# An adaLN transformer block on one core: first norm in natural feature order, key and value weights reordered on PE, a new instruction order

## Chip, cores, metric

The kernel runs on 1 core of a Trainium2 chip. The metric is the device time of one execution in microseconds, the median of several runs. All times below come from those runs or from one profiled execution.

## What is computed

One transformer block on 2048 tokens of width 1024, in bf16, conditioned on a vector `c`:

```
mod = silu(c) @ w_mod                       # six vectors of 1024: sa, ca, ga, sb, cb, gb
h = layernorm(x) * (1 + ca) + sa
q = h @ wq   (32 heads of 32);  k = h @ wk;  v = h @ wv      # one key and value head for all
x = x + ga * (softmax(q k^T / sqrt(32)) v) @ wo
h = layernorm(x) * (1 + cb) + sb
out = x + gb * (silu(h @ w1) * (h @ w3)) @ w2                # inner width 3584
```

## The kernel before

**One static order.** The program describes the work as a graph of operations (`Graph.op`), each with its engine (or alternatives), a duration that the author wrote in, what it reads and writes, and a due value `vt`. `Placer` (lines 194 to 420) then plays the graph in planned time and takes, again and again, the operation that can start first; among those that can start about as early on an engine it takes the lowest due value. Out of this come five fixed instruction streams with semaphore waits. `PLAN` (line 115) is a table with one row for every 16 score steps. A row holds allowances for choosing an operation that starts a little later, a time within which PE shall not change between value runs and fill ("hold"), and additions to the due values by kind of work and engine ("q/pe", "ln/act" and so on). On the chip each engine keeps the order that the planner found, whatever the true durations are. If an operation has alternatives, the engine that can start it first in planned time gets it.

**Setup.** SP issues the loads in this order: token tiles 0 to 3, the first half of w_mod's scale columns (field 1), tiles 4 and 5, the second half, tiles 6 and 7, the first quarter of wq, tiles 8 to 11, the two halves of the shift columns (field 0), the rest of wq, tiles 12 to 15. ACT issues `c`, wk and wv. `WSPL = (0, 4, NC)` (line 589) sets where a field is cut: 8 chunks, 4 and 4.

The width of 1024 is spread over 128 partitions and 8 chunks. In the first norm, feature p*8 + c stands in partition p and chunk c (`pc`, line 573), so that wk and wv (64 bytes a row) can be loaded with 512 bytes a partition. w_mod is loaded in this way too, and so is wq.

- `lnt1` (line 640) handles one tile of 128 tokens: statistics on DVE, 1/sqrt on POOL, normalization on ACT (tiles 0 to 7) or DVE, 8 transposes on PE that take every eighth feature of `XN`, and a copy from PSUM to `HT` on ACT or DVE.
- `mod_cols` (line 673) makes a field's 1024 values as columns: 64 matmuls, for each of 8 chunks and 8 groups of outputs, whose weights are a strided slice of w_mod (every eighth column) and whose moving operand is silu(c), repeated 64 times. Field 1 becomes `MODC` (1 + ca), field 0 becomes `SAB` (sa).
- `scale0` (line 689) multiplies wk, wv (`WKS`) and the first part of wq (`WQ0S`) by 1 + ca. `k_bias` (line 703) makes the biases of K and of the first two groups of Q from `SAB`. `k_proj` (line 741) makes K for 256 tokens, four times over in the partitions, `q_proj` Q, `v_proj` V.
- Two groups of throw-away matmuls on `IDENT` (lines 1076 and 1092, 27 and 16 operations) stand at low priority in between.

**Main stage.** For each of 8 token blocks (256 tokens), 8 groups of 4 heads and 8 pairs of key tiles, `s_exp` (line 834) does a score step: 8 matmuls S (4 heads side by side on the array), then two exponentials on ACT from PSUM to a slot of `U`, a ring of 10 slots. For every 8 steps `av` (line 865) adds the slots up on DVE (pairs, then further levels in `PS`), runs 64 value matmuls over the 8 slots in one go (the value run, U and V), the sums through `ONES`, and normalizes on DVE into `QT`. Between S steps PE gets fill: Q projections, `mod_chunk`, wo (`wo`, line 928), and the feed-forward part (`slab`, `quarter`) of the block before. All fill goes through two PSUM banks, PB. A slot of U can be written again only when its value matmuls and its sums have read it.

**Second norm.** `wo` adds the attention output to x, norms it, and for blocks 1 to 6 transposes by DMA into `QT`; then 8 operations scale and shift the 8 chunks on DVE, planned at 0.17 us each. Blocks 0 and 7 transpose on PE instead.

**Tail.** After the last exponential: the last value run, wo, norm and feed-forward part of block 7.

In the profile nearly all instructions have line 22, a helper; so I name them by engine and tiles. `HT<-PB` on ACT is a tanh of the feed-forward part or, in setup, the copy of a norm.

Of the kernel before, what the change touches and what calls it, by code (L numbers as in the profile page):

```python
# [42 lines left out]
class Graph:  # L43
# [63 lines left out]
    def alias(self, new, old):  # L107
# [8 lines left out]
    (0.0, 0.12, 0.2, 1, 0.7,  # L116
     {"wo/pe": -19, "mc/pe": 25, "slab/dve": -28, "ln/dve": -40, "k/pe": 5, "mod/pe": 114, "mc/dve": 1}),
    (0.0, 0.12, 0.1, 1, 1.3, {"mc/pe": 27, "q/dve": -2, "ln/pe": 6, "ln/act": 32, "v/pe": 15, "mod/pe": 18}),
    (0.0, 0.12, 0.1, 1, 0.9,
     {"mc/pe": 27, "slab/act": -5, "q/dve": -2, "ln/pe": 6, "ln/act": 32, "v/pe": 15, "mod/pe": 18}),  # L120
    (0.0, 0.12, 0.1, 1, 0.9,
     {"q/pe": -119, "mc/pe": 27, "slab/act": -5, "q/dve": -2, "ln/pe": 6, "ln/act": 32, "v/pe": 15, "mod/pe": 18,
      "kb/pe": -44, "mc/dve": -51}),
    (0.0, 0.16, 0.2, 1, 2.6,
     {"slab/pe": -74, "q/pe": 2, "av/dve": 20, "slab/dve": 32, "slab/act": -7, "q/dve": -2, "mc/dve": 6}),
    (0.0, 0.16, 0.2, 1, 1.6,
     {"slab/pe": -74, "q/pe": 2, "av/dve": 20, "slab/dve": 32, "slab/act": -7, "q/dve": -2, "mc/dve": 6}),
    (0.0, 0.16, 0.2, 1, 1.3,
     {"slab/pe": -74, "q/pe": 2, "av/dve": 20, "slab/dve": 32, "slab/act": -7, "q/dve": -2, "mc/dve": 6}),
    (0.0, 0.13, 0.2, 1, 1.3,  # L130
     {"slab/pe": -74, "q/pe": 2, "av/dve": 20, "slab/dve": 32, "slab/act": -7, "wo/dve": 106, "q/dve": -2,
      "mc/dve": 6}),
    (0.0, 0.13, 0.2, 1, 1.3,
     {"slab/pe": -74, "q/pe": 2, "pair/dve": 22, "av/dve": 20, "slab/dve": 49, "slab/act": -7, "wo/dve": 106,
      "q/dve": -2, "mc/dve": 6}),
    (0.0, 0.11, 0.0, 1, 2.4, {"wo/pe": 4, "slab/pe": 107, "quarter/pe": -2, "q/pe": -26, "an/dve": 4, "q/dve": -119}),
    (0.0, 0.11, 0.02, 1, 2.6,
     {"wo/pe": 4, "slab/pe": 107, "quarter/pe": -2, "q/pe": -26, "an/dve": 4, "q/dve": -119}),
    (0.0, 0.11, 0.02, 1, 2.6,
     {"wo/pe": 4, "slab/pe": 107, "quarter/pe": -2, "q/pe": -26, "an/dve": 4, "q/dve": -119}),  # L140
    (0.0, 0.11, 0.2, 1, 2.6,
     {"wo/pe": 135, "quarter/pe": 20, "mc/pe": -8, "pair/dve": 119, "av/dve": -14, "an/dve": 72,
      "quarter/dve": -26, "wo/dve": 65, "q/dve": -66}),
    (0.0, 0.11, 0.2, 1, 1.4, {"wo/pe": -20, "slab/pe": 107, "q/pe": -26, "an/dve": 54, "q/dve": -119}),
    (0.0, 0.11, 0.02, 1, 3.1,
     {"wo/pe": -20, "q/pe": -26, "mc/pe": -3, "av/dve": 8, "an/dve": 54, "slab/dve": 29, "q/dve": -119}),
    (0.0, 0.11, 0.05, 0, 2.3,
     {"av/pe": -15, "q/pe": -9, "mc/pe": 109, "pair/dve": -1, "an/dve": 4, "slab/act": 15, "q/dve": 7,
      "mc/dve": 6}),
    (0.0, 0.11, 0.2, 1, 2.4,  # L150
     {"wo/pe": 17, "quarter/pe": -15, "mc/pe": -8, "pair/dve": -39, "av/dve": 1, "an/dve": 72,
      "quarter/dve": -26, "wo/dve": 65, "q/dve": -72}),
    (0.0, 0.12, 0.2, 1, 1.3, {"slab/pe": -12, "av/dve": 57}),
    (0.0, 0.11, 0.2, 1, 2.9,
     {"av/pe": -12, "wo/pe": -19, "slab/pe": -9, "quarter/pe": -39, "pair/dve": -2, "an/dve": -117,
      "quarter/dve": -16, "q/dve": -105}),
    (0.0, 0.11, 0.2, 1, 1.9,
     {"av/pe": -12, "wo/pe": -19, "slab/pe": -9, "quarter/pe": -39, "pair/dve": -2, "an/dve": -117,
      "quarter/dve": -16, "q/dve": -105}),
    (0.0, 0.11, 0.2, 1, 1.9,  # L160
     {"av/pe": -12, "wo/pe": -19, "slab/pe": -9, "quarter/pe": -39, "pair/dve": -2, "an/dve": -117,
      "quarter/dve": -16, "q/dve": -105}),
    (0.0, 0.11, 0.2, 0, 0.7,
     {"av/pe": -12, "wo/pe": -19, "slab/pe": -9, "quarter/pe": -39, "pair/dve": -2, "an/dve": -143,
      "quarter/dve": -16, "q/dve": -105}),
    (0.0, 0.11, 0.05, 1, 3.1,
     {"wo/pe": -17, "mc/pe": -8, "av/dve": 1, "an/dve": 47, "slab/act": 11, "quarter/dve": -26, "wo/dve": 86}),
    (0.0, 0.11, 0.05, 1, 3.1,
     {"wo/pe": -17, "mc/pe": -8, "av/dve": 1, "an/dve": 47, "slab/act": 11, "quarter/dve": -26, "wo/dve": 86}),
    (0.0, 0.11, 0.05, 1, 3.1,  # L170
     {"wo/pe": -17, "mc/pe": -8, "av/dve": 1, "an/dve": 47, "slab/act": 11, "quarter/dve": -26, "wo/dve": 86}),
    (0.0, 0.14, 0.2, 0, 0.1, {"slab/pe": -12, "pair/dve": -20, "av/dve": -18, "slab/dve": -24}),
    (0.0, 0.11, 0.05, 0, 3.3,
     {"wo/pe": -17, "mc/pe": -8, "pair/dve": 43, "av/dve": 14, "slab/act": 9, "quarter/dve": -26}),
    (0.0, 0.11, 0.05, 0, 3.3,
     {"wo/pe": -17, "mc/pe": -8, "pair/dve": 43, "av/dve": 14, "slab/act": 9, "quarter/dve": -26}),
    (0.0, 0.11, 0.2, 1, 1.4,
     {"av/pe": -15, "quarter/pe": -3, "q/pe": -9, "mc/pe": 33, "pair/dve": -16, "av/dve": -5, "an/dve": 18,
      "quarter/dve": -37, "q/dve": 7, "mc/dve": 6}),
    (0.0, 0.11, 0.2, 1, 1.4,  # L180
     {"quarter/pe": -3, "q/pe": -9, "mc/pe": 33, "av/dve": -5, "an/dve": 18, "quarter/dve": 74, "q/dve": 7,
      "mc/dve": 6}),
    (0.0, 0.11, 0.0, 1, 1.4,
     {"quarter/pe": -3, "q/pe": -9, "mc/pe": 33, "av/dve": -5, "an/dve": 18, "quarter/dve": 74, "q/dve": 7,
      "mc/dve": 6}),
    (0.0, 0.11, 0.05, 0, 4.1,
     {"wo/pe": -17, "slab/pe": -70, "mc/pe": -8, "pair/dve": 43, "av/dve": 14, "slab/dve": 97, "slab/act": 9,
      "quarter/dve": -26}),
    (0.0, 0.11, 0.2, 0, 3.3,
     {"slab/pe": -13, "quarter/pe": 27, "mc/pe": 61, "slab/dve": -16, "quarter/dve": 6, "wo/dve": 2}),  # L190
# [260 lines left out]
def build(nc, x_in, wq_in, wk_in, wv_in, wo_in, w1_in, w3_in, w2_in, c_in, wmod_in, out, S, D, F):  # L451
# [137 lines left out]
    WSPL = (0, 4, NC)  # L589
# [6 lines left out]
    def wq_dma(f0, f1, key, vt):  # L596
        dma("sp", WQ[:, :, f0 * P:f1 * P], pc(wq_in)[:, :, f0 * P:f1 * P], key, (f1 - f0) << 18, writes=[key], vt=vt,
            bw=FAST)
# [20 lines left out]
       reads=["C0", "C2"], writes=["C3"], vt=-1990)  # L619
    op("dve", lambda: [lambda e: e.tensor_copy(WKR[:, 0], WKV[:, 0].unsqueeze(2).broadcast_to([P, NC, 4, 32]))], 0.45,  # L620
# [19 lines left out]
    def lnt1(tt, vt):  # L640
# [286 lines left out]

    def wo(n, vt):
# [16 lines left out]
        if 0 < n < NB - 1:  # L945
# [169 lines left out]
    i = 0  # L1115
# [14 lines left out]
    for k, old in ((1, "WKR0"), (2, "WKR1"), (4, "SABR"), (6, "WQ0S"), (7, "WQ0S"), (5, ("XN", 2))):  # L1130
        G.alias([("PS", k)], [old])
# [73 lines left out]
```

## Time and profile before

| | us |
|---|---|
| median of 3 runs | 1142.18 (1142.15 to 1142.33) |
| profiled execution | 1142.53 |
| its span | 1140.70 |
| PE busy | 1115.7 (98%), 15538 matmuls |
| DVE busy | 953.9 (84%) |
| ACT busy | 1024.3 (90%) |
| POOL busy | 38.3 (3%) |
| exponentials (ACT, U<-S), 1024 | 962.8 busy |
| first exponential starts | 30.97 |
| last exponential ends | 1044.64 |
| granted PE clock | full in all slices |

Busy times of PE are no measure of its limit, since matmuls overlap and their ends are modelled; what counts is where it waits and who waits for it. The DMA share is the mean busy share of 16 DMA engines; it is near 1 in setup and 0.4 to 0.8 after it.

### The profile page before, as it was taken

What the parts mean: (1) busy time and instruction counts of PE and PEld (TensorE: products, weight loads), DVE (VectorE), ACT (ScalarE), POOL (GpSimd) and SP (SyncE); (2) the same over time, 40 slices, a digit from 0 to 9 for tenths busy, and PEclk for the clock granted to TensorE, in tenths of its full rate; (3) what the DMA queues carried; (4) which work ended last, traced back from release to release, by engine and by line L of the source; (5) the groups of instructions that cost most, each with busy time, mean ns of one, the idle gap of its engine ahead of it and who ended that gap; (6) DMA issues with size and microseconds to landing.
All of it is one profiled execution on the core that took longest, in us unless ns stands there. A gap on an engine that the chain in (4) does not pass through costs nothing.

```text
span 1140.7 us, 34695 instructions
## 1 busy us (share of the span) xinstructions
PE 1115.7 (98%) x15538; PEld 756.8 (66%) x15568; DVE 953.9 (84%) x1557; ACT 1024.3 (90%) x1161; POOL 38.3 (3%) x83
## 2 busy tenths in 40 slices
PE   8999999999999999999999999999999999999998
PEld 7644556666577756776567656776577656776887
DVE  7888899998888888888979799888978988888442
ACT  5999999999999999999999999999999999996110
POOL 4100000000000000000000010000100000000000
PEclk9999999999999999999999999999999999999999
DMA  9500379665596668665696659675686658667793
GB/s 345 179 2 1 113 222 245 181 187 155 132 264 194 172 163 221 191 196 154 145 253 196 173 143 236 192 204 131 156 249 192 174 140 231 194 188 202 222 291 118
DMA packets 374291, 209.45 MB, mean 184 GB/s; under 512 B 17536, under 2 KB 365952, under 8 KB 374144
## 3 DMA queue, kind: packets, MB, share of 16 engines
q1 hardware_dynamic: 373712, 207.11, 65.2%
q8 instruction: 122, 2.00, 0.8%
q14 instruction: 25, 0.20, 0.1%
q10 hardware_dynamic: 432, 0.13, 0.0%
HBM read 199.89 MB, written 4.19 MB: 179 GB/s over the span
## 4 chain that ended last, share of the span: by engine, by line
ACT 48%; PE 41%; DVE 8%; DMA 2%; issue 1%; SPq 0%; POOL 0%; DVEq 0%
ACT U L22 44%; PE PB L22 29%; PE S L22 12%; DVE PS L22 4%; ACT HT L22 4%; DVE QT L22 1%; DMA W<-in_A_wq_dram 1%; DVE HT L22 1%; DVE RB L22 1%; DVE X L22 0%; DMA QT<-XNB 0%; SPq L22 0%; DVE ST L22 0%; DVE XNB L22 0%; DVE RC L22 0%
## 5 line engine op out<-in xcount | busy, mean ns | idle before, releaser
L22 ACT ACTIVATE U<-S 128x1024 bf16<-128x1024 f32 x1024 | 962.8, 1105 | 15.7 <-PE S L22 7.7
L22 DVE TENSOR_TENSOR PS<-U 128x2048 bf16<-128x2048 bf16 x256 | 309.1, 1213 | 21.3 <-ACT U L22 19.2
L22 DVE TENSOR_TENSOR PS<-PS 128x1024 bf16<-128x1024 bf16 x368 | 248.9, 685 | 4.0
L22 PE MATMUL PB<-QT,W 128*128 128x256 bf16 x1856 | 230.6, 273 | 0.9 <-DVE RB L22 0.4
L22 PE MATMUL S<-QT,KT 32*128 32x256 bf16 x4096 | 203.4, 273 | 7.8 <-ACT U L22 5.5
L22 PEld LDWEIGHTS PB<-QT,W 128*128 128x128 bf16 x1856 | 169.9, 98 | 49.3 <-issue 26.8
L22 PE MATMUL PB<-W2S,HT 128*128 128x256 bf16 x1512 | 189.8, 273 | 0.0
L22 PEld LDWEIGHTS PB<-W2S,HT 128*128 128x128 bf16 x1512 | 136.9, 98 | 43.8 <-issue 27.2
L22 PEld LDWEIGHTS S<-QT,KT 32*128 32x128 bf16 x4096 | 60.7, 92 | 134.8 <-ACT U L22 122.4
L22 PE MATMUL PB<-U,V 128*32 128x256 bf16 x4032 | 125.6, 273 | 1.6 <-DVE HT L22 1.0
L22 PE MATMUL PB<-QT,HT 128*128 128x256 bf16 x960 | 120.6, 273 | 0.6 <-DVE HT L22 0.3
L22 PEld LDWEIGHTS PB<-U,V 128*32 128x32 bf16 x4032 | 99.7, 96 | 23.4 <-issue 10.8
L22 ACT ACTIVATE HT<-PB 128x512 bf16<-128x512 f32 (+1 forms) x110 | 76.4, 696 | 32.7 <-PE PB L22 32.6
L22 PEld LDWEIGHTS PB<-QT,HT 128*128 128x128 bf16 x960 | 87.7, 98 | 25.8 <-issue 14.0
L22 PE MATMUL PB<-HT,W 128*128 128x256 bf16 (+1 forms) x561 | 98.5, 316 | 2.4 <-issue 1.6
L22 DVE SCALAR_TENSOR_TENSOR HT<-HT,PB 128x512 bf16<-128x512 bf16 x102 | 69.4, 681 | 31.8 <-ACT HT L22 30.9
L22 DVE TENSOR_TENSOR HT<-HT,PB 128x512 bf16<-128x512 bf16 x102 | 69.5, 682 | 15.0 <-PE PB L22 13.2
L22 PEld LDWEIGHTS PB<-HT,W 128*128 128x128 bf16 x576 | 50.2, 97 | 37.0 <-issue 13.9
L22 PE MATMUL PB<-WO,QT 128*128 128x512 bf16 x217 | 54.0, 380 | 1.8 <-issue 1.3
L22 DVE STREAM_TRANSPOSE RB<-PB 128x256 f32<-128x256 f32 x63 | 28.2, 447 | 29.6 <-PE PB L22 29.4
L22 POOL TENSOR_SCALAR RS<-MV 128x1 f32<-128x1 f32 x32 | 11.3, 354 | 1015.4 <-DVE MV L22 1010.4
L22 DVE COPY RB<-PB 128x256 f32<-128x256 f32 x63 | 26.4, 419 | 18.5 <-PE PB L22 18.5
(112 smaller groups left out, 648.9 us busy)
## 6 DMA issues: line engine op xcount, KB each, us to landing
W<-in_B_w_dram SPq DMA_DIRECT2D x150, 512.0 KB, 4.9
W2S<-in_B_w_dram SPq DMA_DIRECT2D x28, 1792.0 KB, 8.3
HT<-in_B_w_dram SPq DMA_DIRECT2D x74, 512.0 KB, 4.9
W2S<-in_w_mod_dram SPq DMA_DIRECT2D x8, 1024.0 KB, 6.8
X<-in_A_x_dram SPq DMA_DIRECT2D x8, 512.0 KB, 6.3
U<-in_w_mod_dram SPq DMA_DIRECT2D x4, 1024.0 KB, 11.4
out_dram<-X SPq DMA_DIRECT2D x7, 512.0 KB, 7.9
U<-in_B_w_dram SPq DMA_DIRECT2D x1, 3584.0 KB, 14.0
```

What stands on the lines that cost most here:

```text
L22: return getattr(e, call[0])(*call[1], **call[2])
```

## The change

1. **Natural order in the first norm.** Feature c*128 + p now stands in partition p and chunk c. wq is loaded in that way (`cp`), the norm's transposes take 128 neighbouring columns, and `mod_cols` takes 128 neighbouring columns of w_mod as weights. Its planned duration goes from 0.482 to 0.23 a chunk. (w_mod's rows, the contraction over `c`, stay in the old order.)
2. **wk and wv** are still loaded in the old order. 8 + 8 transposes on PE put them into rows of 32 partitions, two copies on ACT or DVE with a strided read reorder them, 8 + 8 transposes bring them back, and one copy writes `WKV`. Banks 2, 3 and 4 and two tiles of `PS` serve as room for it.
3. **WSPL** is (0, 6, 8): the first load of a field has 6 chunks, the second 2.
4. **The second norm's 8 scalings** are planned at 0.258 us, and POOL is an alternative, planned at 0.8.
5. **PLAN** is another table, again with 33 rows; every row differs. The instruction order is thus made anew over the whole kernel.

```diff
-    dma("act", WKV[:, i], pc(w), ("WKV", i), 65536, writes=[("WKV", i)], vt=-1999)
+    dma("act", WKV[:, i], pc(w), ("WKV", i), 65536, writes=[("WKL", i)], vt=-1999)
...
-    WSPL = (0, 4, NC)
+    WSPL = (0, 6, NC)
...
-        dma("sp", WQ[:, :, f0 * P:f1 * P], pc(wq_in)[:, :, f0 * P:f1 * P], key, (f1 - f0) << 18, writes=[key], vt=vt,
+        dma("sp", WQ[:, :, f0 * P:f1 * P], cp(wq_in)[:, :, f0 * P:f1 * P], key, (f1 - f0) << 18, writes=[key], vt=vt,
...
+    WT = [PS[:, 3].rearrange("p h q -> p (h q)"), PS[:, 5].rearrange("p h q -> p (h q)")]
+    for i in range(2):
+        op("pe", lambda i=i: [lambda e, c=c: e.transpose(BANKH[2 + i][0:32, c * P:(c + 1) * P], WKV[:, i, c, :], IDENT[:])
+                              for c in range(NC)], 0.53, reads=[("WKL", i), "IDENT"], writes=[("S", 2 + i)], vt=-1990,
+           mode="F", post=0.145)
+        op("act", lambda i=i: [lambda e: e.activation(
+            WT[i][0:32, :].rearrange("p (q c) -> p q c", c=NC), BANKH[2 + i][0:32, :].rearrange("p (c q) -> p q c", q=P),
+            ACT.Copy)], 1.1, reads=[("S", 2 + i)], writes=["WT"] if i == 0 else ["WT1", ("XN", 2)], vt=-1990,
...
+    for i in range(2):
+        op("pe", lambda i=i: [lambda e, c=c: e.transpose(
+            BANKH[4][:, (8 * i + c) * 32:(8 * i + c + 1) * 32], WT[i][0:32, c * P:(c + 1) * P], IDENT[0:32, 0:32])
+            for c in range(NC)], 0.53, reads=["WT" if i == 0 else "WT1", "IDENT"] + ([] if i == 0 else [("XN", 2)]),
+           writes=[("S", 4)], vt=-1990, mode="F", post=0.145, waw=(i == 0))
+    op("act", lambda: [lambda e: e.activation(WKV[:], BANKH[4][:, 0:512].rearrange("p (s c f) -> p s c f", s=2, f=32),
+                                              ACT.Copy)], 0.6, reads=[("S", 4)], writes=[("WKV", 0), ("WKV", 1)], vt=-1990,
...
-                BANKH[b][:, cc * P:(cc + 1) * P], XN[slot].rearrange("p (q c) -> p c q", c=NC)[:, cc, :],
+                BANKH[b][:, cc * P:(cc + 1) * P], XN[slot][:, cc * P:(cc + 1) * P],
...
-                BANK[b][:, 64 * k:64 * k + 64], WM0[:, c, fld * D:(fld + 1) * D].rearrange("p (q k) -> p k q", k=NC)[:, k, :],
+                BANK[b][:, 64 * k:64 * k + 64], WM0[:, c, fld * D + k * P:fld * D + (k + 1) * P],
...
-                for c in range(WSPL[h], WSPL[h + 1]) for k in range(NC)], 0.482 * (WSPL[h + 1] - WSPL[h]), reads=["C3", ("WM0", fld, h)],
+                for c in range(WSPL[h], WSPL[h + 1]) for k in range(NC)], 0.23 * (WSPL[h + 1] - WSPL[h]), reads=["C3", ("WM0", fld, h)],
...
-                   0.17, reads=[("h2r", n, 0), ("h2r", n, 1), ("MODC", 3, cc // 4), ("MODC", 2, cc // 4)],
-                   writes=[h2k(n)[cc]], vt=vt)
+                   0.258, reads=[("h2r", n, 0), ("h2r", n, 1), ("MODC", 3, cc // 4), ("MODC", 2, cc // 4)],
+                   writes=[h2k(n)[cc]], vt=vt, alts=[("pool", lambda cc=cc: [lambda e: e.tensor_scalar(
+                       h2t(n)[:, cc, :], h2t(n)[:, cc, :], MODC[:, 3, cc:cc + 1], MODC[:, 2, cc:cc + 1], ALU.mult,
+                       ALU.add)], 0.8)] if POOLH else [])
```

One row of the table of before and one of after, the first of each:

```
    (0.0, 0.12, 0.2, 1, 0.7,
     {"wo/pe": -19, "mc/pe": 25, "slab/dve": -28, "ln/dve": -40, "k/pe": 5, "mod/pe": 114, "mc/dve": 1}),
...
    (0.2, 0.03, 0.0, 0, 1.4,
     {"q/pe": -9, "slab/act": -80, "wo/dve": -71, "ln/pe": -112, "ln/act": 31, "k/pe": 3, "k/dve": 33}),
```

More of the change, by code (lines that the diff above doesn't have):

```diff
@@ new lines @@
+    (0.0, 0.16, 0.02, 0, 0.7, {"wo/pe": 106, "q/pe": -45, "q/dve": -74, "ln/pe": -118, "ln/dve": 4, "mod/pe": -24}),
+    (0.0, 0.16, 0.02, 0, 0.7, {"wo/pe": 106, "q/pe": -45, "q/dve": -74, "ln/pe": -118, "ln/dve": 4, "mod/pe": -24}),
+    (0.2, 0.24, 0.2, 1, 0.6, {"q/pe": 47, "mc/pe": 46, "ln/act": -12, "k/pe": 22}),
+    (0.0, 0.12, 0.2, 0, 1.8,
+     {"wo/pe": -44, "quarter/pe": 47, "q/pe": 33, "mc/pe": 36, "pair/dve": -14, "wo/dve": -1, "ln/act": -12,
+      "k/pe": 22}),
+    (0.0, 0.11, 0.2, 1, 1.5, {"q/pe": 47, "mc/pe": 46, "av/dve": 6, "ln/act": -12, "k/pe": 22}),
@@ new lines @@
+    (0.0, 0.11, 0.2, 1, 1.9, {"q/pe": -13, "mc/pe": 46, "av/dve": 4, "ln/act": -12, "k/pe": 22}),
+    (0.0, 0.11, 0.2, 0, 3.4, {"wo/pe": 35, "an/dve": 55, "slab/dve": 1}),
+    (0.0, 0.11, 0.2, 1, 1.4, {"av/dve": -11, "an/dve": 55, "slab/dve": 1, "q/dve": 9}),
+    (0.0, 0.11, 0.1, 0, 2.4,
+     {"wo/pe": 14, "slab/pe": 12, "quarter/pe": 3, "q/pe": -6, "av/dve": 18, "an/dve": 69, "slab/act": -1,
+      "quarter/dve": -7}),
+    (0.0, 0.11, 0.05, 0, 2.4, {"slab/act": 6, "wo/dve": 53}),
+    (0.0, 0.11, 0.2, 0, 2.9, {"wo/pe": 46, "an/dve": 55, "slab/dve": -89, "q/dve": 67}),
@@ new lines @@
+    (0.0, 0.11, 0.2, 1, 1.3, {"wo/pe": -13, "pair/dve": 6, "an/dve": 55, "slab/dve": -89, "q/dve": 67}),
+    (0.0, 0.11, 0.1, 1, 2.7,
+     {"slab/pe": -132, "q/pe": 47, "mc/pe": 46, "pair/dve": -13, "av/dve": 23, "slab/dve": -39, "slab/act": -20,
+      "quarter/dve": -47, "ln/act": -12, "k/pe": 22}),
+    (0.0, 0.11, 0.1, 1, 2.3,
+     {"slab/pe": -132, "q/pe": 47, "mc/pe": 46, "pair/dve": -13, "av/dve": -84, "slab/act": -20,
+      "quarter/dve": -47, "ln/act": -12, "k/pe": 22}),
+    (0.0, 0.11, 0.2, 1, 4.1,
+     {"wo/pe": 138, "slab/pe": -132, "quarter/pe": 13, "q/pe": 47, "mc/pe": 46, "pair/dve": -13, "av/dve": -83,
+      "slab/dve": -39, "slab/act": -20, "quarter/dve": -47, "ln/act": -12, "k/pe": 22}),
@@ new lines @@
+    (0.0, 0.11, 0.2, 1, 1.3,
+     {"slab/pe": -124, "q/pe": 47, "mc/pe": 46, "pair/dve": -24, "av/dve": -89, "an/dve": -26, "slab/dve": -39,
+      "slab/act": -20, "ln/act": -12, "k/pe": 22}),
+    (0.0, 0.11, 0.05, 1, 3.7,
+     {"wo/pe": -5, "quarter/pe": 48, "pair/dve": -3, "av/dve": -2, "slab/act": -7, "wo/dve": 20}),
+    (0.0, 0.11, 0.05, 1, 3.7,
+     {"wo/pe": -5, "quarter/pe": 48, "pair/dve": -3, "av/dve": -2, "slab/act": -7, "wo/dve": 20}),
+    (0.0, 0.11, 0.2, 1, 2.6,
+     {"wo/pe": 112, "slab/pe": -124, "quarter/pe": 26, "q/pe": 20, "mc/pe": 46, "pair/dve": 13, "av/dve": -89,
+      "an/dve": -26, "slab/dve": -39, "slab/act": -20, "quarter/dve": 35, "wo/dve": -2, "ln/act": -12,
+      "k/pe": 22}),
@@ new lines @@
+    (0.0, 0.11, 0.2, 1, 1.3,
+     {"slab/pe": -124, "quarter/pe": 26, "q/pe": 52, "mc/pe": 46, "pair/dve": 13, "av/dve": -72, "an/dve": -26,
+      "slab/dve": -39, "slab/act": -20, "quarter/dve": 35, "wo/dve": -6, "ln/act": -12, "k/pe": 22}),
+    (0.0, 0.11, 0.05, 1, 2.6,
+     {"slab/pe": -124, "quarter/pe": 26, "q/pe": 20, "mc/pe": 46, "av/dve": -89, "slab/dve": -39,
+      "slab/act": -20, "quarter/dve": 35, "ln/act": -12, "k/pe": 22}),
+    (0.0, 0.11, 0.05, 1, 1.4,
+     {"slab/pe": -124, "quarter/pe": 26, "q/pe": 20, "mc/pe": 5, "av/dve": -89, "slab/act": -20,
+      "quarter/dve": 35, "ln/act": -12, "k/pe": 22}),
@@ L1129, in build @@
     G.alias([("PS", 0)], [("WKV", 0), ("WKV", 1), "WKS"])
-    for k, old in ((1, "WKR0"), (2, "WKR1"), (4, "SABR"), (6, "WQ0S"), (7, "WQ0S"), (5, ("XN", 2))):
+    for k, old in ((3, "WT"), (1, "WKR0"), (2, "WKR1"), (4, "SABR"), (6, "WQ0S"), (7, "WQ0S"), (5, ("XN", 2))):
         G.alias([("PS", k)], [old])
```

103 lines of the change are left out of this document (29 added, 74 removed).

## The prediction

> **What bounds the kernel now.** I read the windows view first, cutting the span where the exponentials begin and end (ACT, U<-S). Columns: stretch, its length, busy time of PE, PEld, DVE, ACT and POOL with instruction counts, PE clock, DMA share, GB/s.
>
> ```profile
> 0.00:31.00 31.00, 25.72 (x322) 22.61 (x323) 23.59 (x57) 18.70 (x20) 15.50 (x43) 1.00 0.97 342
> 31.00:200.00 169.00, 161.05 (x2463) 88.30 (x2478) 152.19 (x266) 168.13 (x187) 5.04 (x12) 1.00 0.42 125
> 200.00:400.00 200.00, 197.94 (x2848) 133.82 (x2847) 174.97 (x276) 196.52 (x226) 1.91 (x4) 1.00 0.67 184
> 400.00:600.00 200.00, 197.92 (x2763) 131.97 (x2766) 173.86 (x278) 195.33 (x223) 4.64 (x8) 1.00 0.70 189
> 600.00:800.00 200.00, 197.32 (x2837) 134.58 (x2839) 173.48 (x272) 195.00 (x221) 3.59 (x4) 1.00 0.66 180
> 800.00:1000.00 200.00, 198.02 (x2789) 133.74 (x2795) 175.46 (x282) 197.64 (x227) 6.06 (x8) 1.00 0.70 192
> 1000.00:1044.64 44.64, 44.59 (x656) 31.80 (x649) 40.64 (x61) 44.64 (x51) 0.00 (x0) 1.00 0.60 164
> 1044.64:1140.70 96.06, 93.12 (x881) 80.00 (x880) 39.66 (x70) 8.37 (x15) 1.58 (x4) 1.00 0.79 223
> ```
>
> The reader sees three stages. Setup (31.0 us) has its DMA share at 0.97. Main (1013.6 us) has ACT busy for 168.13 + 196.52 + 195.33 + 195.00 + 197.64 + 44.64 = 997.3 us, so it idles 16.4; PE is busy almost as long, and DVE is not the bound. In the tail (96.1 us) PE has all the work: its matmuls run end to end from 1061 on. So the end is the start of the exponentials + ACT's work + ACT's idle + the tail.
>
> Second, the timeline of setup: PE's rows, the cast that makes SAB, and the first exponential (start, length, engine, what, in brackets what it waited for). The DMA line is that of the two loads of shift weights; the later one was issued at 12.0 and has the largest of the three figures.
>
> ```profile
> 23.50 2.08 PE L22 MATMUL PB<-SCC,U 128*128 128x64 bf16 x32
> DMA to landing us min/median/max: 12.4/13.2/13.9
> 25.93 2.08 PE L22 MATMUL PB<-SCC,U 128*128 128x64 bf16 x32
> 28.14 0.11 DVE L22 CAST SAB<-PB 128x8 bf16<-128x8 f32 x1
> 28.60 0.66 PE L22 MATMUL PB<-SAB,W 128*128 128x64 bf16 x16
> 30.49 0.40 PE L22 MATMUL S<-QT,KT 32*128 32x256 bf16 x8
> 30.97 1.93 ACT L22 ACTIVATE U<-S 128x1024 bf16<-128x1024 f32 x2
> ```
>
> The second half of the shift weights lands at 12.0 + 13.9 = 25.9, and PE starts on it at 25.93. From there to the first exponential there is a single chain: 32 matmuls, the cast, the bias matmuls, the bias, K and Q, the scores. That chain, and not the norm, starts the main stage.
>
> Third, where ACT idles in the main stage. Its gaps listed one by one come to 14.8 us in 18 places; three of them, 2.69 us before 301.00, 2.38 before 587.14 and 1.65 before 622.33, wait for PE's PB matmuls. PE and ACT around the first:
>
> ```profile
> 298.92 1.70 PE L22 MATMUL PB<-W2S,HT 128*128 128x256 bf16 x14
> 300.55 1.93 PE L22 MATMUL PB<-U,V 128*32 128x256 bf16 x64
> 301.00 1.94 ACT L22 ACTIVATE U<-S 128x1024 bf16<-128x1024 f32 x2 [2.69 <-PE PB L22]
> ```
>
> The exponential at 301.00 had its scores (S ran at 297.65). It waited for a free slot of U, and the 64 value matmuls that read the oldest slots were put behind 14 feed-forward matmuls. The other two gaps have the same shape (26 and 22 fill matmuls, then the 64). So the main stage loses time where the order on PE puts a value run late.
>
> **The change, part by part.** The profiled execution took 1142.53 us (span 1140.70, 1.83 around it); the median of the runs is 1142.18, so I add up against 1142.53 and take 0.35 off.
>
> (a) Modulation columns, packed weights and a 6:2 split. Packed and strided loads stand beside each other in the groups:
>
> ```profile
> L22 PEld LDWEIGHTS PB<-SCC,U 128*128 128x128 bf16 x128 | 8.1, 165 | 0.9 <-DMA U<-in_w_mod_dram 0.9
> L22 PEld LDWEIGHTS PB<-SCC,W2S 128*128 128x128 bf16 x256 | 8.6, 98 | 1.7 <-issue 1.3
> ```
>
> The U form is strided by 8 elements, the W2S form packed, with the same 128 x 64 matmul behind both. In busy time a strided one costs 8.1/128 = 63 ns, a packed one 8.6/256 = 34. After the change the last piece holds 2 of 8 chunks, so 2 x 8 = 16 matmuls come after the landing. The first piece, 6 chunks, lands when 0.52 MB are still to come, at the 374 to 379 GB/s of that time 1.4 us earlier, at 24.5; its 48 packed matmuls take 48 x 34 ns = 1.6 and end at 26.1, a little past the landing. Sixteen packed matmuls of this shape took 0.66 (at 28.60): 26.8, and the cast 0.13 behind as now, at 26.9 instead of 28.14: -1.2 us. The bytes ahead of the landing are the same, in descriptors of the same length, so I leave 25.9 as it is. Bounds: -1.4 (PE done with the 48 at the landing) and 0.
>
> [...]
>
> (b) First S. K and Q are ready at 29.97, but PE does another K projection from 29.51 until S at 30.49, so a new order can gain up to 0.5 here; I take -0.2. Against (a) and (b) stands what comes next: the last two K blocks need token tiles 12 to 15, whose load was issued at 16.8 and lands 15.8 later, at 32.6, and their S steps run at 43.10 and 44.94. An earlier ACT could run dry there. From tile 12's landing to its K block I count 0.1 + 1.3 (statistics, two tiles: +1.5) + 0.2 + 1.0 (POOL) + 0.5 + 0.5 + 1.0 + 1.05 + 0.5, about 40.3, and the S that needs it ran at 43.1. So 2.8 us of room. Setup in sum: -1.4, from 0 (room not used) to -1.9.
>
> (c) Key and value weights: 32 transposes, three copies. Eight norm transposes take 0.5 us on PE, so 2.0 us; PE fills that time with 48 throw-away matmuls until 8.4, which hide them. The copies cost by the nearest rows 1.02 + 1.02 + 0.6 = 2.6 us on ACT (0.67, 0.67, 0.67 on DVE). The loads land at 4.9 and 6.8, the chain of the second ends near 10, and its first reader runs at 14.20: 4 us of cover. ACT idled 3.98 us before its first norm at 7.63. Value 0, bounds 0 and +2.6 (if the copies push the norms back one for one and these become last).
>
> (d) Norm transposes, packed: in busy time 72 ns a load against the 34 above, but the matmul behind takes 56 to 62. 128 of them gain at most 128 x 6 ns = 0.8 us on a PE that waits for loads: 0.
>
> (e) Second norm's scaling: 48 operations, on DVE or POOL, planned at 0.258 (0.17 before).
>
> ```profile
> 308.11 2.13 DVE L22 TENSOR_SCALAR QT<-QT,MODC 128x256 bf16<-128x256 bf16 x8
> 17.87 1.95 POOL L22 TENSOR_SCALAR PS<-W,MODC 128x256 bf16<-128x256 bf16 x2 [2.20 <-DMA W<-in_A_wq_dram]
> ```
>
> On DVE 2.13/8 = 0.266 each, on POOL 1.95/2 = 0.98 for the same shape. The planner gives an operation to whoever starts first, so POOL takes about 2 of 8 (1.95 us) while DVE does 6 (1.6): the block is ready in 2 us as now. DVE loses 12 x 0.266 = 3 us of work that bounds nothing. Value 0. Bounds: -1 (the order fits the true 0.266), +11 if POOL took 4 of 8: 4 x 0.98 - 2.13 = 1.8 us late, six blocks.
>
> (f) The new order. The table again has 33 rows; what it does in the main stage cannot be read off. The nearest rows are the kernel's own five stretches from 31 to 1000: idle 0.9, 3.5, 4.7, 5.0, 2.4 (standard deviation 1.7, so sqrt(5) x 1.7 = 3.8 on their sum). An order of the same quality would give 16.4 +/- 3.8; the ends are 0 idle (-16.4) and every stretch like the worst (5 x 5.0 = 25, +8.6). I take -2.4, one late value run fewer, because two durations that the planner had wrong (0.17 for 0.266; 1.93 for 2.08) are now near the rows, and such an order slips less on the chip.
>
> (g) Tail. The 448 + 224 feed-forward matmuls of the last block (0.109 each, 73.2 us) and what must come before them do not change. What could go is 1.0 us (the last value run starts at 1045.66, behind fill, where its exponentials end at 1044.64) and 0.7 (six left-over matmuls at 1102); what could come is more left-over fill, 18 matmuls for 2 us. Value 0, bounds -1.7 and +2.
>
> Sum: -1.4 - 2.4 = -3.8, so 1138.7 for a profiled execution and 1138.4 for the median.
>
> **Rivals.** 0.2% is 2.3 us, about what a measurement of this kernel can tell from no change: faster is below 1139.9, slower above 1144.5.
>
> Rival 1. Order much better: main idle halves, -8.2 - 1.4, so 1132.6. For it: the gaps are few and large. Against: PE is busy 198 of 200 us, with little room to move fill.
>
> Rival 2. Nothing arrives: the setup gain is given back at the later K blocks, or the new order costs what setup gains: 1140.8 to 1142.2. For it: a spread of 3.8 in (f) is larger than the gain.
>
> Rival 3. Slower by late value runs: each costs (2.69 + 2.38 + 1.65)/3 = 2.2 us, where 14 or more fill matmuls stand between an S and a value run while U is full. The new order is made anew everywhere, so it can have more than three. It decides from two more: 1142.2 - 1.4 + 4.4 = 1145.2; three more, 1147.4.
>
> Rival 4. Slower by POOL blocking DVE. If a POOL scaling shuts DVE out, 12 x 0.98 = 11.8 us are lost and 3.2 saved, at six places where PE waits for this very block: 1142.2 - 1.4 + 8.6 = 1149.4. Against: beside the two POOL operations at 17.87 six DVE scalings took 1.71 us, where eight alone take 2.13 (six, 1.6): 0.1 lost, not 1.95. [...]
>
> **Chances.** Forecast 0.50 (1136 to 1139.9), rival 1 0.16, rival 2 0.20, rival 3 0.09, rival 4 0.05. Faster: 0.50 + 0.16 + 0.01 of rival 2 = 0.67; the same 0.19; slower 0.14. The range takes in rivals 1 and 2 and the worse half of (f): 1132.6 to 1144.5; it leaves out the slower cases and a little beyond rival 1.
>
> **What to look for.** Right if the SAB cast falls near 26.9, the first exponential near 29.6, the strided loads' mean of 165 ns is gone, ACT's idle between first and last exponential is near 14, and the tail stays at 96. Wrong if the cast is late (landing moved, or PE behind the new transposes), if an exponential waits between 36 and 45 us, if more than three gaps wait for a value run, or if the DVE operations beside POOL's scalings stretch.

## The result, and the profile after

The changed kernel took 1134.4 us (median of 4 runs, 1133.84 to 1134.48), the kernel before 1142.16 beside it: a ratio of 0.9931, 95% interval 0.9916 to 0.9947, so 7.8 us less. The forecast was 1138.4. In what follows PE is the matrix engine, ACT ScalarE, DVE VectorE and POOL GpSimd; a score step, or S, is the group of matmuls that feeds two exponentials, and a value run the 64 matmuls that read eight slots of `U`. The profiled execution has a span of 1132.6 us against 1140.70.

The windows view of the changed kernel, cut again where its exponentials begin and end (same columns as in the prediction):

```profile
0.00:30.61 30.61, 23.94 (x354) 19.18 (x355) 22.94 (x57) 20.85 (x23) 15.83 (x43) 1.00 0.98 345
30.61:200.00 169.39, 163.05 (x2484) 87.51 (x2486) 151.42 (x265) 168.66 (x188) 6.23 (x12) 1.00 0.43 125
200.00:400.00 200.00, 198.53 (x2867) 135.79 (x2868) 177.18 (x276) 198.42 (x227) 4.95 (x6) 1.00 0.68 185
400.00:600.00 200.00, 199.21 (x2838) 134.59 (x2837) 176.01 (x279) 197.27 (x225) 10.10 (x12) 1.00 0.71 192
600.00:800.00 200.00, 199.51 (x2807) 134.49 (x2804) 176.20 (x274) 197.27 (x225) 5.77 (x8) 1.00 0.68 185
800.00:1000.00 200.00, 199.28 (x2869) 137.18 (x2866) 176.13 (x278) 198.63 (x229) 9.37 (x11) 1.00 0.70 190
1000.00:1036.50 36.50, 36.45 (x518) 25.86 (x516) 32.42 (x51) 36.50 (x42) 0.00 (x0) 1.00 0.60 164
1036.50:1132.60 96.10, 93.16 (x882) 80.04 (x880) 39.61 (x70) 8.36 (x14) 1.59 (x4) 1.00 0.81 223
```

Setup is 0.4 us shorter (30.97 to 30.61) and the tail is what it was (96.06, now 96.10). The main stage fell from 1013.67 to 1005.89. ACT's busy time in it is 168.66 + 198.42 + 197.27 + 197.27 + 198.63 + 36.50 = 996.75, as before (997.3); its idle time fell from 16.4 to 9.1. The gain is idle time of ACT in the main stage: -7.3, with -0.4 at the start and -0.5 of ACT work. The -0.4 is no more than the scatter of single profiles, as b_pool below shows.

What ACT's exponentials waited for in the main stage (us in total, times, longest), first in the kernel before, then in the changed one:

```profile
ACT U L22 <- PE S L22: 7.7, 14, 1.4
ACT U L22 <- PE PB L22: 6.7, 3, 2.7
```

```profile
ACT U L22 <- PE S L22: 8.8, 8, 1.4
```

The three waits for late value runs (PB) are gone. What is left are six gaps of 1.36 us, one in each of blocks 2 to 7. The first of them, in the timeline of the changed kernel:

```profile
278.73 0.40 PE L22 MATMUL S<-QT,KT 32*128 32x256 bf16 x8
279.06 1.48 PE L22 MATMUL PB<-W2S,HT 128*128 128x256 bf16 x12
280.47 1.93 PE L22 MATMUL PB<-U,V 128*32 128x256 bf16 x64
282.33 0.40 PE L22 MATMUL S<-QT,KT 32*128 32x256 bf16 x8
282.78 1.02 ACT L22 ACTIVATE U<-S 128x1024 bf16<-128x1024 f32 x1 [1.36 <-PE S L22]
```

Between two S steps stand 12 fill matmuls and a value run, 3.4 us, in which ACT uses up its scores. The value run is on time here; it is the next S that comes late.

From the first exponential of a token block to that of the next, in us (blocks 0 to 6), worked out from counts of the exponentials:

```
before   123.15 124.95 128.37 127.00 130.29 127.81 125.39
after    123.09 125.70 126.13 126.13 126.19 126.13 126.13
```

The new order does the same thing in every block from the third on, to within 0.1 us; the old one varied by 5 us.

The setup rows that answer to those in the prediction:

```profile
23.50 0.62 PE L22 MATMUL PB<-IDENT,XNB 128*128 128x128 bf16 x8 [0.60 <-ACT XNB L22]
25.54 2.16 PE L22 MATMUL PB<-SCC,U 128*128 128x64 bf16 x64 [0.29 <-ACT HT L22]
27.50 0.19 DVE L22 BATCH_NORM_AGGREGATE MV<-ST 128x2 f32<-128x12 f32 x1
27.74 0.17 DVE L22 CAST SAB<-PB 128x8 bf16<-128x8 f32 x1
30.61 1.93 ACT L22 ACTIVATE U<-S 128x1024 bf16<-128x1024 f32 x2
```

A packed shift matmul takes 2.16/64 = 34 ns, as forecast from the packed rows. But all 64 ran in one go from 25.54, and the cast came at 27.74, not at 26.9.

### The profile page after: what moved, and what is told of

It is laid out like the page before. It is cut to its first block, busy times and chain, and to the rows that moved or that the text cites. A ratio compares the mean times of both kernels' runs of the same rounds, so it can differ in the third digit from the quotient of the medians.

```text
span 1132.6 us, 34805 instructions
## 1 busy us (share of the span) xinstructions
PE 1113.1 (98%) x15600; PEld 754.6 (67%) x15600; DVE 951.9 (84%) x1544; ACT 1026.0 (91%) x1165; POOL 53.8 (5%) x95
## 4 chain that ended last, share of the span: by engine, by line
PE 63%; ACT 31%; DVE 4%; DMA 1%; issue 0%; POOL 0%; SPq 0%; DVEq 0%
PE PB L22 47%; ACT U L22 30%; PE S L22 16%; DVE PS L22 2%; DMA W<-in_A_wq_dram 1%; ACT HT L22 1%; DVE HT L22 1%; DVE RB L22 0%; SPq L22 0%; DVE ST L22 0%; DVE W L22 0%; ACT XNB L22 0%; POOL PS L22 0%; DVE XNB L22 0%; POOL RS L22 0%
## 5 line engine op out<-in xcount | busy, mean ns | idle before, releaser
L22 PE MATMUL PB<-HT,W 128*128 128x256 bf16 (+1 forms) x576 | 101.8, 318 | 1.0 <-DVE HT L22 0.6
L22 PE MATMUL PB<-WO,QT 128*128 128x512 bf16 x232 | 57.3, 381 | 0.0
L22 ACT ACTIVATE HT<-S 128x512 bf16<-128x512 f32 (+1 forms) x15 | 10.9, 736 | 30.5 <-PE S L22 30.5
```

The lines of the kernel that those rows point to most:

```text
L22: return getattr(e, call[0])(*call[1], **call[2])
```

## The experiments

The theory to be tested (theory 1 in the expectations): the gain is the order of PE's instructions in the main stage, and it holds only for the graph it was planned for. Its main rival there (theory 3): the edited operations (packed loads, scalings on POOL) bring the gain in any order. Besides, each term of the sum was tried alone. Where it says "order fixed", the planner's order was recorded and the program written out in that order with one edit; the figures in brackets behind a time are its ratio to the kernel before, measured beside it, and the 95% interval of that ratio. The kernel after has 1134.4 and a ratio of 0.9931. It ran only beside the first measurement of before, 1142.16; beside the experiments before took 1142.21 (the two tables, a_respaced, a_late_runs), 1142.62 (a_scal_dve, a_strided, a_split44, a_no_reorder) and 1142.61 (the other four). So a difference from 1134.4 below about 0.5 us says nothing, and the ratios are the safer guide.

**Table and graph exchanged.** The kernel before with the new table, and the changed kernel with the old one.

```diff
 # b_new_table, in the kernel before
-PLAN = [ 33 rows of before ]
+PLAN = [ 33 rows of after ]
```

> The kernel before with the new table alone, all else as before; the planner makes a new order from it. Theory 1 (the gain is this one order in the main stage, and a table is worth something only with the graph and durations it was found for): the order it gives leaves 102.3 us of planned PE work after the last score step where before has 96.1, and has 17 stretches with a value run that are over 2.3 us long, where before has five over 3; at 1 to 2 us each and 6 us of tail this is 1155 to 1170. Theory 2 (the new table is the better one by itself): about 1135. Theory 3 (the gain is the new setup and the true durations, whatever the table): about 1142.

Measured: 1172.51 (ratio 1.0265, 1.025 to 1.028), 2.5 above the range that theory 1 gave. ACT idles 36.3 us in its main stage, where before has 16.4, and the tail takes 103.1 us.

```diff
 # a_old_table, in the kernel after
-PLAN = [ 33 rows of after ]
+PLAN = [ 33 rows of before ]
```

> The changed kernel with the old table: natural order, packed weights, 6:2 split, transposes of the key and value weights, scalings at 0.258 and on POOL all stay. Theory 1 (the gain is this one order): the order it gives leaves 115.5 us of planned PE work after the last score step (96.1 in both kernels), so the tail is about 19 us longer while the main stage has 19 us less fill and can end earlier only as far as ACT allows (about 8 us at most): 1143 to 1155. Theory 3 (the gain is the new setup and the true durations, whatever the table): about 1134 to 1137.

Measured: 1161.18 (1.0164, 1.0149 to 1.0179), also beyond the range that theory 1 gave. Here ACT idles 16.3 us, as in before, and the tail takes 116.2 us, 20 more than in either kernel. Either mixture is 19 to 38 us slower than either kernel. So the edited operations do not bring the gain whatever the order (theory 3 falls as the whole cause), and neither of these two tables is worth anything away from its graph.

**The twelve scalings back on DVE** (a_scal_dve, order fixed).

```diff
 # the 12 operations that the planner gave to POOL (chunks 1 and 5 of six blocks)
-n.alt = 1   # pool
+n.alt = 0   # dve, in the planned sequence
```

> The changed kernel's order, held fixed, with the 12 second-norm scalings that run on POOL put back on DVE at the same place. My reading of the change (POOL's share bounds nothing): 1134.4 within 0.5. Rival (taking 3 us off DVE, or getting the block's first chunks earlier, is part of the gain): +2 to +4 us. Rival (POOL shuts DVE out while it runs): the kernel gets faster without it, by up to 8 us.

Measured: 1136.76 (0.995, 0.9935 to 0.9965), 2.4 us slower than after, or 2.2 by the ratios. That alone is little more than the two intervals allow, but the trace bears it out: blocks of 126.5 instead of 126.13, and 11.3 us of idle time on ACT in the main stage instead of 9.1. The waits of ACT, the place in the timeline where the wait arises, and the same place in after:

```profile
ACT U L22 <- PE S L22: 11.0, 14, 1.4
```

```profile
438.20 0.68 DVE L22 SCALAR_TENSOR_TENSOR HT<-HT,PB 128x512 bf16<-128x512 bf16 x1
438.94 1.93 PE L22 MATMUL PB<-U,V 128*32 128x256 bf16 x64 [0.34 <-DVE HT L22]
440.80 0.40 PE L22 MATMUL S<-QT,KT 32*128 32x256 bf16 x8
441.25 1.02 ACT L22 ACTIVATE U<-S 128x1024 bf16<-128x1024 f32 x1 [0.36 <-PE S L22]
```

```profile
437.75 0.68 DVE L22 SCALAR_TENSOR_TENSOR HT<-HT,PB 128x512 bf16<-128x512 bf16 x1
438.48 1.93 PE L22 MATMUL PB<-U,V 128*32 128x256 bf16 x64
```

The two extra scalings (0.53 us) hold up DVE's SCALAR_TENSOR_TENSOR from 437.75 (in after) to 438.20. That operation empties a PB bank, the value run waits for the bank, S stands behind the value run, and ACT runs dry for 0.36 us: six times 0.36 is the 2.2 that its waits grew by. DVE is idle for 12% of the block and still sets the end here.

**The same edit the other way round** (b_pool, the kernel before, order fixed).

```diff
 # chunks 1 and 5 of the eight scalings, six blocks
-q["dve"]
+q["pool"]
```

> The kernel before in its own order, with chunks 1 and 5 of the eight scalings in each of six blocks moved from VectorE to GpSimd, as after has them. If moving them is worth the 2.2 us that the reverse edit cost in after wherever it is done: 1140.0. If the worth came only from after's order, which was planned around the shorter VectorE work: within 0.6 of before, 1141.6 to 1142.8. If GpSimd's slower scalings (about 1.1 us each) come late for the fill that reads them: 1143 to 1146.

Measured: 1140.97 against 1142.61 (0.9985, 0.9976 to 0.9995), so -1.6, with an interval from -0.6 to -2.7: in the old order, too, the scalings on POOL are worth something, with no table made for them. ACT's waits in it:

```profile
ACT U L22 <- PE PB L22: 6.7, 3, 2.7
ACT U L22 <- PE S L22: 6.1, 9, 1.4
```

S waits fell by 1.6 and the three late value runs stayed. With this, -1.6 to -2.4 of the 7.8 belong to the scalings. What the order is worth without POOL stands in a_scal_dve, which has the new order and all scalings on DVE: against before it is 5.7 us faster (0.995), and ACT's idle time is 11.3 instead of 16.4. So about -5 of the main stage's gain is the order's.

This run also shows how far single profiles of one setup differ, for its setup is that of before, unchanged:

```profile
27.85 0.11 DVE L22 CAST SAB<-PB 128x8 bf16<-128x8 f32 x1
30.69 1.93 ACT L22 ACTIVATE U<-S 128x1024 bf16<-128x1024 f32 x2
```

In before's own profile these stood at 28.14 and 30.97. With after's setup, the first exponential starts at 30.61 in after, 30.33 in a_scal_dve and 30.86 in a_respaced_less. So the 0.4 us between before and after at the start of the exponentials cannot be told from nothing.

**Late value runs** (a_late_runs, order fixed, one in each of six blocks; the score steps after each are spaced anew).

```diff
 # PE, at six value runs
-S, 64 value matmuls, S, fill and S ...
+S, 12 fill matmuls, 64 value matmuls, S, fill and S ...
```

> The changed kernel's order, held fixed, with one edit on PE: six value runs in mid-block (heads' groups 20, 28, 36, 44, 52, 60) are put behind 12 fill matmuls that stood after them, and the score steps after them are spaced so that nothing else moves. This puts back, six times, the shape of the three long gaps of the kernel before (2.69, 2.38, 1.65 us of ACT idle). If a late value run costs its gap, +1.4 to 2.2 us each, +8 to +13: 1143 to 1147. If PE alone sets the pace of a block, its instructions are the same and the end stays: 1134 to 1136, with ACT's idle time up all the same.

Measured: 1152.48 (1.009, 1.0075 to 1.0105): 18.1 us, 3.0 for each, more than the 2.2 that the three gaps of before gave, and above both expected results. From its timeline:

```profile
362.82 1.93 PE L22 MATMUL PB<-U,V 128*32 128x256 bf16 x64
364.68 0.40 PE L22 MATMUL S<-QT,KT 32*128 32x256 bf16 x8
365.13 2.85 ACT L22 ACTIVATE U<-S 128x1024 bf16<-128x1024 f32 x3 [1.93 <-PE S L22]
367.86 0.62 ACT L22 ACTIVATE HT<-PB 128x512 bf16<-128x512 f32 x1
368.51 0.69 DVE L22 SCALAR_TENSOR_TENSOR HT<-HT,PB 128x512 bf16<-128x512 bf16 x1
369.34 0.60 PE L22 MATMUL PB<-QT,W 128*128 128x256 bf16 x4 [1.54 <-DVE HT L22]
370.32 1.02 ACT L22 ACTIVATE U<-S 128x1024 bf16<-128x1024 f32 x1 [0.93 <-PE S L22]
```

The first gap (1.93) also delays the tanh, with it DVE's operation behind the tanh, and with that the bank that PE wants next: PE waits 1.54 us, and ACT gets a second gap of 0.93. In this edit a gap is paid one and a half times. Two things limit the comparison with before: ACT waits for scores here, not for a slot of U as at the three gaps of before, and the score steps that were spaced anew lie between the first gap and the second, so the 0.93 may be theirs in part; no run takes this apart.

**The six gaps spread out** (a_respaced, order fixed: 16 S steps around each gap spaced evenly in planned time).

```diff
 # PE, around each 1.36 us gap
-S, 12 fill, value run, S, 4 fill, S ...
+S steps at equal distances of planned PE time between the same fill and value runs
```

> The changed kernel's instruction order, held fixed, with one edit on PE: at the six places where ACT idles 1.36 us (a score step stands behind 12 fill matmuls and a value run, once in each of blocks 2 to 7), the 16 score steps from there on are spaced evenly among the same other instructions. Theory 1a (PE and ACT are tied at about 126 us a block, and the six gaps are only where PE's full load shows): the gaps on ACT go or shrink, the end moves by 0 to -3 us: 1131.5 to 1134.5. Rival 1b (ACT alone is the limit, and the six gaps are faults of the order): -8.2 us, about 1126.

Measured: 1138.46 (0.9967, 0.9955 to 0.9978), 4.1 slower than after; both expected results were missed. The 1.36 gaps are gone, and others stand in their place:

```profile
ACT U L22 <- PE PB L22: 5.4, 6, 0.9
ACT U L22 <- PE S L22: 3.7, 8, 0.8
```

Moving S steps ahead means moving the value run back, and the U slots then come free 0.9 us late. This is only part of the loss: the main stage is 4.3 us longer than in after (1010.21 against 1005.89), of which 1.6 is idle time of ACT and 2.7 is busy time of ACT (999.46 against 996.75), for the same 1130 instructions. Why they take longer is open.

**The respaced order with less fill** (a_respaced_less): is it the amount of PE's work that leaves no room?

```diff
-for f in range(f0, f0 + 2)]
+for f in range(f0, f0 + (1 if f0 < 16 and q == 1 and not last else 2))]
```

> The respaced kernel (after's order, the S steps evenly spread at the six gaps; 1138.5, blocks of 126.8) with 16 of the 56 matmuls of one feed-forward quarter left out in blocks 0 to 6, so about 2.0 us less fill per block at 0.123 us each; that part of the sum is left out of the output. If PE's own work bounds a block (125.80 busy of 126.82): blocks shrink by 1.4 to 1.7 to 125.2 to 125.4, where ACT's 125.2 busy ends it, and the whole is 9 to 11 us shorter than the respaced one, about 1128 to 1130. If the bound is the chain of bank releases (PB waits, 0.9 each, one per block) and not the amount of work: blocks stay within 0.4 of 126.8 and the time is 1136 to 1138.5.

Measured: 1139.75 (0.9976, 0.9966 to 0.9986), no faster than the respaced kernel; blocks of 126.82 to 127.19, and the six PB waits as in it. One row of the windows view tells why; it is the second half of a block, first in the respaced kernel, then in this one:

```profile
470.00:533.00 63.00, 62.85 (x916) 44.31 (x918) 56.75 (x88) 63.00 (x74) 0.00 (x0) 1.00 0.62 174
```

```profile
470.00:533.00 63.00, 61.48 (x901) 42.60 (x902) 56.76 (x87) 63.00 (x74) 0.00 (x0) 1.00 0.62 174
```

PE lost 1.4 us of work there, and ACT was busy for 63.00 of 63.00 in both. Most of the omitted matmuls stood where ACT was already full; the gaps lie before 470, in the first half of the block. So PE at 99% does not bound the block as a whole by the amount of its work: over the main stage PE lost 10 us of work (13.7 us idle became 23.6) and the end did not move. ACT is busy for nearly the whole block, and what it loses it loses at the places where the order leaves it without scores or slots; the time freed here was not carried there. Leaving out fill right at those places was not tried.

**Strided loads back** (a_strided, order fixed; it permutes scale and shift among features).

```diff
-WM0[:, c, fld * D + k * P:fld * D + (k + 1) * P]
+WM0[:, c, fld * D:(fld + 1) * D].rearrange("p (q k) -> p k q", k=NC)[:, k, :]
```

> The changed kernel's order, held fixed; only the two modulation columns made in setup read their weights with a stride of 8 again (this permutes the scale and shift, a changed computation of the same size). If the packed loads are worth their time (34 against 63 ns), the 64 matmuls that stand in one piece before the shift's cast take 1.9 us longer, cast and first exponential move from 27.7 and 30.6 to 29.6 and 32.5, and the end follows by +1 to +1.9: 1135.5 to 1136.5. If setup has 2 us of cover elsewhere, 1134.4.

Measured: 1137.29 (0.9953, 0.9936 to 0.9969), +2.9, or 2.5 by the ratios; more than the 1 to 1.9 expected. Its shift matmuls and cast:

```profile
26.30 4.05 PE L22 MATMUL PB<-SCC,U 128*128 128x64 bf16 x64 [0.29 <-ACT HT L22]
30.39 0.17 DVE L22 CAST SAB<-PB 128x8 bf16<-128x8 f32 x1 [2.86 <-PE PB L22]
```

4.05/64 = 63 ns against 34: the two durations that the prediction read from busy times hold. Here the cast waits 2.86 us for PE, so the strided loads are paid in full: the cast stands 2.65 us later than in after, and so does the first exponential (33.26). Of this 1.89 is the longer run of 64, as expected; the other 0.76 was there when the run began (26.30 against 25.54). The scale columns, made earlier, are strided here too, which is a likely reason; that was not taken apart.

**Packed loads alone, in the old order** (b_packed, order fixed; the same two lines exchanged in the kernel before, which permutes features likewise).

> The kernel before in its own order, its modulation weights read in packed slices (128 neighbouring elements) instead of every eighth, which permutes scale and shift among features: the output is of permuted features. With 63 ns a strided load and 34 ns a packed one, the last 32 shift matmuls take some 0.9 us less: the cast at 27.2 to 27.3 instead of 28.14, the first exponential 0.8 to 0.9 earlier at about 30.1, the whole 1141.3. If the first scores wait for something else than the cast (the norm tiles): no change, 1142.2.

Measured: 1142.68 against 1142.61 (1.0001, 0.9992 to 1.001): no gain that can be seen. Its last shift matmuls and DVE's rows up to the cast:

```profile
25.56 1.17 PE L22 MATMUL PB<-SCC,U 128*128 128x64 bf16 x32
26.04 1.23 DVE L22 BATCH_NORM_STATS2 ST<-W2S 128x6 f32<-128x512 bf16 x2
27.19 0.53 DVE L22 TENSOR_SCALAR XNB<-W2S,MV,RS 128x1024 bf16<-128x1024 bf16 x1
27.64 0.20 DVE L22 BATCH_NORM_AGGREGATE MV<-ST 128x2 f32<-128x12 f32 x1
27.76 0.11 DVE L22 CAST SAB<-PB 128x8 bf16<-128x8 f32 x1
```

The matmuls end at 26.73, and the cast runs at 27.76, with no idle time on DVE: it stands in DVE's queue behind the norm statistics of later token tiles. (The 0.38 by which it is earlier than before's 28.14 was there at 21.28 already, where ACT's norm stood at 21.66 in before; and b_pool, with the strided loads, has its cast at 27.85.) In the kernel before, matmuls (28.01) and queue ended almost together, so only one of them could be seen.

**The shift columns out of the line** (a_own_bank, order fixed): a bank of their own, ahead of the second norm transposes.

```diff
-PE: norm tile 6, norm tile 7, 64 shift matmuls (PB)
+PE: norm tile 6, 64 shift matmuls (S bank 4), norm tile 7
```

> The kernel after in its own order, with the shift's 64 weight-stationary matmuls and their cast moved to PSUM bank 4 of their own and put ahead of the second norm tile's transposes, so that they no longer wait for the HT copies of ACT that empty the shared PB bank. Theory (the cast came late because the matmuls waited in line, not because of the loads): the matmuls start soon after the weights' landing at about 24.4 and 25.9, the cast stands at 26.8 to 27.0 instead of 27.74, the first exponential near 29.7 to 29.9 instead of 30.61, and the whole is 0.7 to 0.9 us shorter than after, 1133.5. Rival (the norm tiles, not the shift columns, set the first scores): the cast is early, the first exponential stays at 30.5 or comes later because the norm's transposes now stand behind the matmuls, and the time is 1134.4 to 1135.5.

Measured: 1135.08 (0.9934, 0.9918 to 0.9951), 0.7 above after, or 0.3 by the ratios, so no difference that can be told from none. In its profile the first exponential stands at 31.43, 0.8 later than in after. The theory named there fell:

```profile
24.55 2.16 PE L22 MATMUL S<-SCC,U 128*128 128x64 bf16 x64 [0.28 <-DMA U<-in_w_mod_dram]
27.73 0.20 DVE L22 BATCH_NORM_AGGREGATE MV<-ST 128x2 f32<-128x12 f32 x1
27.85 0.11 DVE L22 CAST SAB<-S 128x8 bf16<-128x8 f32 x1
```

The matmuls were done a micro-second earlier, at 26.71, and the cast still came at 27.85, behind the same DVE work. The rival's time came out, but not by its way, for the cast was not early. What came later is behind the cast: eight transposes that PE runs before the bias matmuls waited for ACT's copy until 28.37, where in after they ran at 27.55.

**The 6:2 split** (a_split44, order fixed).

```diff
-WSPL = (0, 6, NC)
+WSPL = (0, 4, NC)
```

> The changed kernel's order, held fixed; the modulation loads are cut 4:4 again instead of 6:2. In the changed kernel all 64 matmuls of the shift start in one piece at 25.54 behind a PSUM bank that a norm tile holds, about when the last bytes land, so I expect the 6:2 split to be worth 0 to 0.5 us: 1134.4 to 1134.9. If the split itself is what counts, 16 more matmuls wait for the last bytes: +0.6 us or more.

Measured: 1134.6 (0.9929, 0.9915 to 0.9944): the split is worth nothing, since in this order the matmuls start so late that both pieces are there when they are read. In after the two loads, issued at 10.8 and 12.0, landed 13.6 to 13.8 us later, so by 25.8; the matmuls ran from 25.54 at 34 ns each, and by that figure they reach the second piece at 27.2, or at 26.6 with a 4:4 cut.

**No reordering of key and value weights** (a_no_reorder, order fixed; the 32 transposes and three copies are left out, so K and V are made with permuted weights).

```diff
-for i in range(2): op("pe", ... e.transpose(...)); op("act", ... WT[i] ...)
-for i in range(2): op("pe", ... e.transpose(...))
-op("act", ... WKV ...)
```

> The changed kernel's order, held fixed, without the 32 transposes and 3 copies that reorder the key and value weights (they stay in the loaded order, so K and V are made of mismatched features; that part of the computation is left out). If these are hidden beside the loads: 1134.4 within 0.4. If they push the first norms and with them the cast of the shift: up to -2.6 us, with the norms of tiles 0 and 1 about 1 us earlier.

Measured: 1135.76 (1134.03 to 1136.83; ratio 0.9938, 0.9924 to 0.9953). The time is 0.8 above after by the ratios, outside the 0.4 that was expected; the cast came 0.77 later, because the granted PE clock fell (last section). In three of the four runs the clock over the whole execution was 0.997 or 0.998, and these took 1135.22 to 1136.83; in the one in which it was 1.000, as in all four of after, the time was 1134.03. So leaving the work out gains less than 1 us, if anything: it is hidden, as forecast.

## Why the prediction was right in sign and short in size

The end as start + ACT's work + ACT's idle + tail held: ACT's work moved by 0.5, the tail by 0.04. The sign and the range were right, but 1134.4 lies below the forecast's own band (1136 to 1139.9), on the way to rival 1. Three terms were mis-sized: setup brought less than forecast, the scalings and the order more.

(a), (b) Setup, forecast -1.4, measured -0.4, which single profiles cannot tell from 0. The step that failed reads "26.8, and the cast 0.13 behind as now". The 34 ns was right (a_strided shows 63 against 34 with only the stride changed), and so was the first landing (24.5; in a_own_bank PE starts on it at 24.55). But the changed order put all 64 matmuls behind two norm transposes and the copy that empties their bank, and, more basically, the cast is held by DVE's in-order queue until about 27.7, however early PE is done (at 26.73 in b_packed and 26.71 in a_own_bank, with the cast at 27.76 and 27.85). The prediction took the cast's releaser for PE, from one row at which two ends coincided, and never read DVE's rows ahead of it. The packed loads are no gain in the order of before, but they are needed: in the new order strided ones cost 2.5 to 2.9.

(c) Key and value weights: 0 forecast, and a_no_reorder shows no cost. (d) Norm transposes: eight took 0.61 or 0.62 in after and 0.64 to 0.71 in before, which in the mean is 0.07 for a group and 1.1 for sixteen, more than the bound of 0.8, but on a PE that waits there; no run takes this apart.

(e) The scalings: forecast "3 us of work that bounds nothing. Value 0", bounds -1 and +11. Measured -1.6 (old order) and -2.2 to -2.4 (new order), both beyond the bound of -1, though the interval of the first (-0.6 to -2.7) takes the bound in. POOL took exactly the 2 of 8 that were forecast. What failed is the cover. The prediction took DVE's work to bound nothing, because DVE as a whole is not the bound; but a few operations behind the scalings, DVE empties a PSUM bank that PE's next value run waits for (0.34 us before 438.94 in a_scal_dve).

(f) The order: forecast -2.4 ("one late value run fewer"); ACT's idle fell by 7.3, of which 1.6 to 2.4 belong to (e), so the order gave about -5, as a_scal_dve against before shows too. All three late value runs went, 6.7 us of waits, and 1.4 us gaps took back part of it. The step's spread (bounds -16.4 to +8.6) held it; its centre did not. Which entries of the table or which durations brought the even blocks is open: every row changed. Whether the three late runs of before alone could be moved ahead in the old order was not tried.

(g) Tail: 0, measured +0.04.

Rival 1 (main idle halves, 1132.6) was nearest in mechanism: 16.4 to 9.1, with 8.2 as its figure, but its setup gain of 1.4 failed. Rival 2 holds for setup alone, and not for its reason: the gain did not come at all, rather than being given back at the K blocks (in after no exponential waits between 36 and 45 us). Rival 3's price was too low by a_late_runs (3.0 where 2.2 stood, with score steps spaced anew besides), and no value run came late for its slots. Rival 4 is out: taking POOL's scalings away makes the kernel slower, and DVE was not shut out. In after POOL's two ran from 304.93 for 2.22 us; beside them DVE's six took 1.78 us from 305.96, where eight alone take 2.13 in before (six, 1.6). POOL's own scalings vary from 0.60 to 1.73 us in after; why was not tested.

## What to carry to other kernels

Where one engine is busy all the time, count its idle places one by one and ask for each which instruction in which in-order queue came late; work freed elsewhere, even on an engine at 99%, need not move the end, and in the one place tried here it did not. An engine with 12 to 16% idle time is still on the path at each place where it empties a buffer that a full engine waits for, and a step that looks released by one engine may stand in another's queue. A planning table tuned for one graph of operations made the other graph slower here, both ways round, though the planner made a new order each time: tune it again after each edit.

## What the runs showed of the hardware

The granted PE clock was not full throughout every run, and a fall in setup to 0.50 delayed the start by 0.76 us (the first exponential of a_no_reorder stands at 31.37, that of after at 30.61). The windows view of a_no_reorder, and below it the rows of after and of a_respaced_less that answer to its first (columns as above; the figure behind POOL's count is the granted clock):

```profile
18.00:20.00 2.00, 0.33 (x2) 0.14 (x3) 2.00 (x7) 2.00 (x2) 1.90 (x2) 1.00 1.05 387
20.00:22.00 2.00, 2.00 (x18) 1.80 (x19) 2.00 (x7) 0.02 (x2) 0.91 (x3) 0.69 1.06 388
22.00:24.00 2.00, 2.00 (x11) 1.44 (x10) 2.00 (x6) 2.00 (x2) 1.57 (x6) 0.50 1.05 383
```

```profile
18.00:20.00 2.00, 0.51 (x4) 0.31 (x5) 2.00 (x7) 2.00 (x3) 1.71 (x2) 1.00 1.06 388
18.00:20.00 2.00, 0.28 (x1) 0.10 (x1) 2.00 (x7) 2.00 (x3) 1.96 (x2) 1.00 1.05 385
```

In a_no_reorder the clock fell to 0.50 behind a stretch with PE busy for 0.33 us of 2; 15 throw-away matmuls then took 3.00 us instead of 1.80, and the cast came 0.77 later (28.51). In after, with 0.51 of 2, it stayed at 1.00, and in a_respaced_less with 0.28 it did so too, in that stretch and the next. So how little PE did in that stretch does not decide it. PE's longest wait between 12 and 22 us was 1.64 us in a_no_reorder (before 19.95); before has one of 1.58 (before 19.97), and its clock stayed at 1.00. The clock also fell in the main stage: in a_strided to 0.52 (180 to 182 us), where PE's longest wait in the 6 us before was 0.88 us. In after, with the same order and a wait of 0.88 before 177.53, it stayed at 1.00.

The clock over the whole execution was below full in three of the four runs of a_no_reorder (0.997 or 0.998) and in none of after's four; a_strided, which has the hidden transposes too, was at 0.998 in one of its four. Whether the transposes keep the clock up in after was not shown, and what decides the fall is open.
